# One written order for all engines: lists of pieces for the ramp and for each batch of an attention and feed-forward kernel

## The chip, the cores and the metric

The kernel runs on one core of a Trainium2 chip. The metric is the time of one execution on the device in microseconds (us), lower is better. An execution is repeated a few times, and medians and intervals are given. Times "in the trace" come from one profiled execution and count from the start of its span; the span is about 2 us shorter than the measured time of the same execution (before: 399.9 us of span, 401.66 us measured).

The engines are called by their names: TensorE (PE, with its weight loads PEld), VectorE (DVE), ScalarE (ACT), GpSimd (POOL, which here only issues loads), and SyncE (SP, which issues transposes by DMA and the stores).

## The reference

Block-causal attention for 8 batches, 8 heads, 576 positions and head dimension 64 (blocks of 64), then an RMS norm over the 512 concatenated channels and a gated feed-forward layer:

```python
scores = scale * np.matmul(q, k.transpose(0, 1, 3, 2))       # masked by blocks of 64
attn = np.exp(scores - max) / sum
x = np.matmul(attn, v)            # -> 4608 tokens x 512
xn = x / sqrt(mean(x * x) + 1e-6) * rms_g
g = xn @ w_gate                   # 512 -> 1536
out = (g * sigmoid(g) * (xn @ w_val)) @ w_out                # 1536 -> 512
```

Everything is float32 outside and bfloat16 in the matmuls.

## The kernel before

Attention of batch b runs on TensorE interleaved with the feed-forward layer of the batches before it, so that TensorE has other work while ScalarE computes exponentials. The feed-forward work lies in a queue of *pieces*: a gate piece, a value piece or a third of a down projection, each of 4 matmuls of 512 columns (or 8 of 256). A chunk of 512 tokens gives 36 pieces, and it enters the queue ("release") once its tokens are normalised and transposed.

The places that matter: batches 0 and 1 are loaded "wide" (many heads in one load) and transposed on TensorE; later batches are loaded by head and transposed by DMA. The norm of a batch is five squares (ScalarE), an inverse root of about a dozen small VectorE operations, five scales (VectorE), each followed by a DMA transpose into the chunk `XT`.

```python
def norm_squares(b, tiles): ...            # one ScalarE Square per tile, accum_out=ss
def norm_scale(b, tiles):
    def root(): ...                        # 1/sqrt by 3 Newton steps, 12 small VectorE operations
    def one(j, t):
        nc.vector.scalar_tensor_tensor(out=XS[:, j, :], in0=XN[:, t, :], scalar=rs[:, j:j + 1], in1=grow, ...)
        for i, (a, e) in enumerate(chunks):
            ...
            sp(nc.sync.dma_start_transpose(out=xt(i)[:, :, lo - a:hi - a], in_=XS[...]))
...
load_wide(0, 0, 0, 2); load_wide(0, 1, 0, 2)          # queries, keys of heads 0-1 of batch 0
load_wide(0, 0, 2, 4); load_wide(0, 1, 2, 4)
load_v_chunk(0, 0);    load_v_chunk(0, 1)
load_wide(0, 0, 4, H); load_wide(0, 1, 4, H)
...
for hp in range(HP):                                   # the ramp: batch 0, first 256 tokens
    tpose_wide(0, hp)
    early[hp].both(0)
    if hp > 1:
        early[hp - 2].values(0)
...
for s, sl in enumerate(slots):                         # one slot per batch and pair of heads
    ...
    budget = max(0, total - RESERVE) / (nxt - s) ...   # feed-forward pieces for this slot
    for i, f in enumerate(pieces):                     # scores and exponentials, values, ...
        if f: f()
        ...
        left = ffn(left + budget * shares[i] / sum(shares))
    for f in todo + aside + rels.pop(s, []) + pp + loads.pop(s, []):
        f()
```

TensorE, the load queue (POOL) and SyncE are chained to the order in which the program is written; VectorE and ScalarE are ordered by the framework's scheduler.

The softmax here doesn't subtract the row's maximum and nothing guards it: scores larger than these inputs give would overflow.

## Time and profile before

| | before |
|---|---|
| time, median of 4 runs | 400.72 us |
| first feed-forward matmul | 31.0 us |
| first transposes of batch 1 on TensorE | 43.6 us |
| first scores of batch 2 | 72.6 us |
| first scores of batch 3 | 108.1 us |
| one steady batch (first scores to first scores) | 39.66 us |

The page gives busy tenths of 40 slices of 10 us each, for TensorE, for the clock that it was granted, and for the DMA engines:

```profile
PE   2559978986999999999999999999999999999996
PEclk9999999989899999999999999999999999999999
DMA  9999999999979997999899785590050032002002
```

TensorE is full from about 110 us on; what can be won lies before. The DMA engines are busy without a break for the first 110 us. The timeline of TensorE, before (start us, duration us, engine, line, operation, count, and in brackets the idle time just ahead of it and who ended it):

```profile
6.64 1.50 PE L195 MATMUL f<-ident,HT 96*64 96x96 bf16 x24 [6.64 <-DMA HT<-in_q_dram]
...
30.95 1.89 PE L89 MATMUL f<-XT,WG 128*128 128x256 bf16 x8
...
43.63 0.70 PE L195 MATMUL f<-ident,HT 96*64 96x96 bf16 x24
...
72.60 0.61 PE L89 MATMUL s<-QKT 64*128 64x512 bf16 x6
```

The second line is the first feed-forward piece, the third begins batch 1's transposes, the fourth is batch 2's first scores.

### The profile page before, as it was taken

To read this page: it belongs to the slowest core of one execution; us is meant where nothing else is said; L and a number is where in the kernel's file an instruction comes from. 1 tells how busy PE (TensorE), PEld (TensorE's weight loads), DVE (VectorE), ACT (ScalarE), POOL (GpSimd) and SP (SyncE) were. 2 spreads that over 40 slices of the span, in tenths; PEclk is the share of its full clock that TensorE was granted. 3 is DMA by queue.
4 is the path that set the end of the run, shared out by engine and by line. 5 is a ranking of instruction groups with operands and counts; after the bars stand their busy time and mean duration, and the time that the engine had idled before them with its cause. 6 is when DMAs were issued, how large, how long until landed. Compare 5 with 4: busy or idle time off the path is not lost.

```text
span 399.9 us, 7708 instructions
## 1 busy us (share of the span) xinstructions
PE 367.2 (92%) x2924; PEld 187.5 (47%) x2924; DVE 259.3 (65%) x664; ACT 208.7 (52%) x369; POOL 138.0 (35%) x192
## 2 busy tenths in 40 slices
PE   2559978986999999999999999999999999999996
PEld 1337745752444444454445444544445444444442
DVE  6763895665578568846884679467947873742850
ACT  1256666783567466746673667366734622323321
POOL 8743497898059305840692061000000000000000
PEclk9999999989899999999999999999999999999999
DMA  9999999999979997999899785590050032002002
GB/s 119 191 203 186 188 82 163 171 111 131 197 47 88 168 177 49 78 126 223 54 87 171 167 53 36 112 183 2 11 130 29 0 60 107 0 26 80 0 3 103
DMA packets 158597, 41.08 MB, mean 103 GB/s; under 512 B 145120, under 2 KB 153824, under 8 KB 158560
## 3 DMA queue, kind: packets, MB, share of 16 engines
q0 software_dynamic: 103840, 18.89, 61.7%
q1 hardware_dynamic: 54720, 21.70, 26.7%
q8 instruction: 23, 0.38, 0.4%
q14 instruction: 14, 0.11, 0.1%
HBM read 38.01 MB, written 9.44 MB: 119 GB/s over the span
## 4 chain that ended last, share of the span: by engine, by line
PE 70%; DVE 12%; ACT 11%; issue 3%; DMA 3%; POOL 1%; DVEq 0%; POOLq 0%; ACTq 0%
PE f L89 65%; ACT sq L340 5%; PE s L89 4%; ACT PT L258 3%; DVE th L426 2%; ACT th L425 2%; DVE HT L432 2%; DMA HT<-in_k_dram 2%; DVE QK L198 2%; DVE XN L306 1%; DMA XT<-XS 1%; DVE XS L356 1%; POOL HT L80 1%; DVE PT L268 1%; DVE y L320 1%
## 5 line engine op out<-in xcount | busy, mean ns | idle before, releaser
L89 PE MATMUL f<-XT,WG 128*128 128x512 bf16 (+1 forms) x480 | 112.9, 363 | 3.7 <-DMA XT<-XS 2.3
L89 PE MATMUL f<-XT,WV 128*128 128x512 bf16 (+1 forms) x480 | 113.2, 364 | 0.0
L425 ACT ACTIVATE th<-f 128x512 f32<-128x512 f32 x108 | 64.2, 596 | 84.2 <-PE f L89 76.4
L426 DVE SCALAR_TENSOR_TENSOR th<-th,f 128x512 f32<-128x512 f32 x108 | 74.0, 685 | 52.0 <-ACT th L425 51.2
L89 PE MATMUL f<-WO,HT 128*128 128x512 bf16 x432 | 99.7, 379 | 1.8 <-DVE XN L306 1.5
L258 ACT ACTIVATE PT<-s 128x1024 bf16<-128x1024 f32 x88 | 86.9, 1023 | 10.8 <-PE s L89 10.7
L432 DVE TENSOR_TENSOR HT<-th,f 128x512 bf16<-128x512 f32 x108 | 74.1, 686 | 8.8 <-PE f L89 1.8
L89 PEld LDWEIGHTS <-WG 128*128 128x128 bf16 x480 | 45.4, 99 | 47.8 <-issue 6.4
L80 POOL DMA_DIRECT2D VN<-in_v_dram x48 | 38.7, 854 | 82.9 <-PE f L89 76.8
L89 PEld LDWEIGHTS <-WV 128*128 128x128 bf16 x480 | 45.1, 99 | 44.1 <-issue 4.0
L89 PEld LDWEIGHTS <-HT 128*128 128x128 bf16 x432 | 39.8, 98 | 46.3 <-issue 2.9
L446 ACT ACTIVATE ob<-f 128x512 f32<-128x512 f32 x36 | 21.5, 597 | 71.7 <-PE f L89 69.7
L80 POOL DMA_DIRECT2D QKN<-in_q_dram x60 | 49.0, 816 | 5.0 <-DMA WO<-in_moe_w_out_dram 3.4
L80 POOL DMA_DIRECT2D QKN<-in_k_dram x60 | 48.7, 812 | 5.1 <-DMA WO<-in_moe_w_out_dram 2.1
L89 PEld LDWEIGHTS <-PT 128*128 128x128 bf16 x960 | 40.1, 100 | 20.2 <-DVE PT L268 4.9
L89 PE MATMUL f<-VN,PT 128*128 128x65 bf16 x960 | 44.1, 198 | 4.8 <-DVE PT L268 4.0
L268 DVE MEMSET PT<- 64x64 uint32 (+1 forms) x124 | 12.8, 114 | 44.1 <-ACT PT L258 39.9
L306 DVE TENSOR_TENSOR XN<-f,rd 128x320 f32<-128x320 f32 (+2 forms) x64 | 31.2, 489 | 1.3
L359 DVE SCALAR_TENSOR_TENSOR XS<-XN,y,grow 128x512 bf16<-128x512 f32 x35 | 24.9, 745 | 0.7
L340 ACT ACTIVATE sq<-XN 128x512 bf16<-128x512 f32 x40 | 25.0, 625 | 0.3
L89 PE MATMUL s<-QKT 64*128 64x512 bf16 (+4 forms) x240 | 22.5, 298 | 1.0 <-ACT PT L258 1.0
L89 PEld LDWEIGHTS <-QKT 64*128 64x128 bf16 (+1 forms) x264 | 10.4, 95 | 25.1 <-issue 22.2
(41 smaller groups left out, 139.3 us busy)
## 6 DMA issues: line engine op xcount, KB each, us to landing
out_dram<-ob SPq DMA_DIRECT2D x36, 256.0 KB, 2.6
VN<-in_v_dram POOLq DMA_DIRECT2D x32, 128.0 KB, 4.2
QKN<-in_k_dram POOLq DMA_DIRECT2D x48, 64.0 KB, 3.7
QKN<-in_q_dram POOLq DMA_DIRECT2D x48, 64.0 KB, 3.5
WG<-in_moe_w_gate_dram POOLq DMA_DIRECT2D x4, 384.0 KB, 10.8
WV<-in_moe_w_val_dram POOLq DMA_DIRECT2D x4, 384.0 KB, 11.5
WO<-in_moe_w_out_dram POOLq DMA_DIRECT2D x2, 768.0 KB, 10.6
XT<-XS SPq DMA_TRANSPOSE x39, 3.5
```

Source lines behind the costliest of these rows:

```text
L80: return chain("POOL", nc.gpsimd.dma_start(**kw))
L89: pe(nc.tensor.matmul(dst, w, r, start=start, stop=stop))
L198: nc.vector.tensor_copy(out=T[:, n, :].rearrange("p (j s) -> p j s", s=SLOT), in_=t[:, 0:S].rearrange("p (s j) -> p j s", s=SLOT))
L258: nc.scalar.activation(out=PT[:, a0:a0 + T4], in_=st, func=AF.Exp, scale=SM_SCALE)
L268: nc.vector.memset(blk[:, :, 0:BLK], 0.0)
L306: nc.vector.tensor_tensor(out=xn_tiles[self.b][:, t0:t0 + n, f0:f0 + m * D].rearrange("p t (h d) -> p h t d", h=m), in0=xv[:, :, :, 0:D], ...
L340: nc.scalar.activation(out=sq, in_=XN[:, t, :], func=AF.Square, accum_out=ss[:, j:j + 1])
L359: nc.vector.scalar_tensor_tensor(out=XS[:, j, :], in0=XN[:, t, :], scalar=rs[:, j:j + 1], in1=grow, op0=ALU.mult, op1=ALU.mult)
L425: nc.scalar.activation(out=th, in_=pg, func=AF.Tanh, scale=0.5)
L426: nc.vector.scalar_tensor_tensor(out=th, in0=th, scalar=1.0, in1=pg, op0=ALU.add, op1=ALU.mult)
L432: nc.vector.tensor_tensor(out=ht, in0=gates.pop((i, k)), in1=pv, op=ALU.mult)
L446: nc.scalar.mul(out=ob, in_=po, mul=0.5)
```

## The change

The intent is to fix the order of every engine, and to shorten the ramp. Slots and budgets go; the program is a text of tokens per batch, in which `F` is one feed-forward piece, `A0`, `B1`, ... are sessions of scores and exponentials, `V00`, ... values, `q0`-`q4`, `r`, `c0`-`c4` the squares, root and scales (each with its transpose) of the batch before, `z` its release, `l` one prefetch load and `p` one transpose of queries and keys. VectorE and ScalarE are chained as TensorE was.

```diff
+    RAMP = """
+    F T0 F T1 F T2 F E0 E1 M1 M0 F T3 E2 e0 E3 e2 D00 F e1 F D10 e3 n0 Z n1 nr F D01 Z D02 nx M2 L0
+    D11 F K0 Z M3 Z F nt K2 F F D03 F K1 a0 F F D22 F D13 D12 D20 F D21 F F D23 a1 D31 t0 D30 K3
...
+    SECOND = """
+    F v0 p v1 A0 F q4 F q1 p F F q0 F F q2 F B1 F F q3 F F F F r c2 F F l c0 c1 V00 c3 F V01 C1 F F
+    F F F l l l F F F A2 F V10 p l F V11 l B3 l c4 z F F F p l C3 F F l l F l F F l l V20 V21 l F F
+    """
+    STEADY = """          (the same text as SECOND)
+    END = """
+    v1 v0 F q4 q3 F F F q0 F q2 q1 F r F c3 c4 F F c1 F F c2 c0 z
+    """
...
+    class Ordered:
...
+            return lambda *a, **kw: chain(self.key, f(*a, **kw))
+    dve = Ordered("DVE", nc.vector)
+    act_ = Ordered("ACT", nc.scalar)
...
-            nc.vector.tensor_copy(out=T[:, n, :]...            # query and key copies
+            copy = act_.copy if n == 0 else dve.tensor_copy    # queries to ScalarE
...
-    load_wide(0, 0, 0, 2)
     load_wide(0, 1, 0, 2)
+    load_wide(0, 0, 0, 2)
...
+    for h in (4, 6):
+        load_wide(0, 1, h, h + 2)
+        load_wide(0, 0, h, h + 2)
+    for c in range(NC):
+        load_v_chunk(0, c)
```

Batch 0's first squares and scales are split between VectorE and ScalarE, its root loses one operation, two large clears become small ones, and four matmuls on zeros (`Z`) are put into the ramp.

## The prediction

> **What bounds the kernel now.** TensorE, everywhere but at the front. The windows view has it busy 39.5 to 39.7 of each 40 us from 160 to 360 us, and the chain of waits repeats every 39.67 us per batch. Priced at the warm rates of the trace (a 512-column matmul 0.216 us apart, a values matmul 0.041), the work between 110 and 390 us loses only some 5 us. By the same count (an estimate from those durations) about 43 us are lost before 110 us: 23 until the first feed-forward matmul at 31.0 us, 10 more until batch 2's scores at 72.6, 10 more until 110. Only these can be won; some 4 us at the end (last eviction and store) stay.
>
> Inside them the timeline shows: the first load landing at 6.60 us; query and key copies of 0.76 us, two in a row on VectorE, before each score; squares of batch 0 on ScalarE behind exponentials (22.7 to 24.6), a root of twelve small VectorE operations mixed with masks (24.7 to 28.3), scales to 29.5; 128x256 feed-forward matmuls in eights at 1.89 us until 36 us where later ones take 1.05. The Trainium skill, "TensorE: Matmul & The Clock Gate", Part 1, says an idle TensorE is clocked at half rate and needs about 3.4 us of activity to warm; these numbers agree, and the granted clock falls to 0.50 in 84 to 86 us after waits for exponentials.
>
> **What the change does.** It removes no matmul and adds four 512-column ones (zeros, about 1 us, in idle time). Half of the 16 query/key copies go to ScalarE; the two 1.47 us clears become small ones; batch-0 squares are split over VectorE and ScalarE, the root loses one operation and its interruptions, scales split over two engines. Key loads go first, in two-head pieces, values after them. All engine orders become fixed. Feed-forward pieces per batch: 21 in the ramp, 25 in batch 2 (its queue runs dry for 12 list entries until batch 1 is released), 36 after, 11 plus 87 at the end.
>
> **Size, step by step** (estimates from the durations above). Batch 0's last early values finish near 18 instead of 21.9 us; squares 0.8, root about 2.1, scale 0.6, transposes and copies 1.5: first feed-forward matmul at 23.5 us instead of 31.0, so -7.5. From there the loads limit: wide keys of batch 1 land at 38.5 us and down-projection weights at 45.5 and 49.7 in the old trace, with queues that hold the same bytes; the transposes of batch 1 begin near 38.5 instead of 43.6, and batch 2 near 65 instead of 72.6. Batch 2 without feed-forward pieces in its middle is bound by ScalarE's exponentials of about 1 us: I expect 6 us lost there instead of 10. Steady batches: the period changes by under 0.5 us. Nearly all of the ramp's gain is on the critical path, since everything after is TensorE in order. Sum: about -12 us, so 388.5 us (range 382.5 to 394.5). Chances: faster 0.84, same 0.14, slower 0.02.
>
> **What would show it.** First feed-forward matmul at 22 to 26 us; batch-1 transposes at 37 to 41; batch 2's first scores at 62 to 68; a thin stretch of TensorE in batch 2; batch period 39.2 to 39.9; the tail after the last scores at the warm 0.86 us per four matmuls. DMA busy share of the ramp unchanged.
>
> **What would make it wrong.** Values of batch 0 landing later than about 14 us, behind all keys and queries; the fixed order putting a late operation before an urgent one on VectorE or ScalarE; a cold clock in batch 2's thin stretch; or steady batches that gain (or lose) a microsecond each.

## More of the kernel before

SyncE's own timeline in batch 2, before:

```profile
91.28 7.70 SPq L367 DMA_TRANSPOSE XT<-XS  x6
99.34 1.25 SPq L208 DMA_TRANSPOSE QKT<-QKN  x1
```

and of the group of instructions that touch `XT` between 60 and 110 us, before, the wait and the time from issue to landing of the six transposes:

```profile
  DMA XT<-XS: 2.3, 1
...
DMA to landing us min/median/max: 4.3/4.6/5.1
```

TensorE waits 2.3 us for the normalised batch 1. (Next to each transpose, loads of queries and keys were in flight here too; those of the values of batch 3 had landed by 89.4 us.)

## The result

| | before | after |
|---|---|---|
| time, median of 4 runs each | 400.72 us | 396.57 us (396.10 to 396.88) |
| ratio | | 0.9894, 95% interval 0.9874 to 0.9915 |
| first feed-forward matmul | 31.0 | 23.9 |
| first transposes of batch 1 | 43.6 | 38.6 |
| first scores of batch 2 | 72.6 | 68.4 |
| first scores of batch 3 | 108.1 | 109.4 |
| steady batch | 39.66 | 39.00 |

The change is about 1% faster, clear of the noise but under 2%, a third of what was predicted, and outside the range.

The page, after, in the same three rows:

```profile
PE   2888879973999999999999999999999899999996
PEclk9999999995999999999999999999999999999999
DMA  8999999999999999977999691760140031002002
```

The first slices are fuller, and a hole has opened in the ninth and tenth (79 to 99 us), with the clock at half speed in the tenth. The timeline of TensorE, after:

```profile
6.81 4.46 PE L224 MATMUL f<-ident,HT 96*64 96x96 bf16 x72 [6.81 <-DMA HT<-in_k_dram]
...
23.93 1.96 PE L117 MATMUL f<-XT,WG 128*128 128x256 bf16 x8
...
38.62 0.70 PE L224 MATMUL f<-ident,HT 96*64 96x96 bf16 x24
...
68.40 0.61 PE L117 MATMUL s<-QKT 64*128 64x512 bf16 x6
...
95.21 0.59 PE L117 MATMUL f<-XT,WG 128*128 128x512 bf16 x1 [7.51 <-DMA XT<-XS]
96.02 1.06 PE L117 MATMUL f<-XT,WG 128*128 128x512 bf16 x2 [0.22 <-issue]
96.87 1.91 PE L117 MATMUL f<-XT,WV 128*128 128x512 bf16 x4
...
100.59 1.03 PE L117 MATMUL f<-XT,WV 128*128 128x512 bf16 x4
```

TensorE has run all fifteen pieces that the queue still held and most of batch 2's attention by 87.7 us, and then waits 7.51 us for the transposed activations of batch 1. The pieces after the wait take 1.91 us for four matmuls until the clock is back, where later ones take 1.03. SyncE's timeline and the `XT` group (60 to 110 us), after:

```profile
82.01 1.19 SPq L414 DMA_TRANSPOSE XT<-XS  x1
83.30 0.53 SPq L512 DMA_DIRECT2D out_dram<-ob  x1
83.92 6.50 SPq L414 DMA_TRANSPOSE XT<-XS  x4
```

```profile
  DMA XT<-XS: 7.5, 1
...
DMA to landing us min/median/max: 4.1/7.6/8.7
```

The transposes are issued 9 us earlier than before (82.0 against 91.3), but the slowest now takes 8.7 us to land instead of 5.1. TensorE's next chunk needs the first four of the six: the fourth was issued at 86.99 us and landed at 95.07, and the wait ended at 95.21.

**Where the gain went.** The two kernels do not do the same work between the same marks, so the lead has to be corrected for it: one feed-forward piece (4 weight loads) is 0.863 us at the warm pace, and two groups of values are 1.07 us. At batch 2's first scores both have done 152 feed-forward weight loads, and the changed kernel has two value groups more. At batch 3's it has 20 weight loads (5 pieces) and two value groups more; at the last values, 8 weight loads (2 pieces) more.

| mark | before | after | extra work done, after | lead of after |
|---|---|---|---|---|
| first scores of batch 2 | 72.60 | 68.40 | 1.1 us | 5.3 us |
| first scores of batch 3 | 108.12 | 109.40 | 5.4 us | 4.1 us |
| first scores of batch 7 | 266.80 | 265.38 | 5.4 us | 6.8 us |
| last values | 308.89 | 303.40 | 1.7 us | 7.2 us |
| end of span | 399.9 | 394.7 | none | 5.2 us |

So the ramp wins 5.3 us, batch 2 loses 1.2, the four steady batches from 3 to 7 win 2.7, batch 7 itself 0.4, and the end loses 2.0.

The end: the last list puts the root and the scales of batch 7 on VectorE between gate and value pieces, whose products then stand behind them (timeline of TensorE, after):

```profile
312.87 1.02 PE L117 MATMUL f<-XT,WG 128*128 128x512 bf16 x4 [0.65 <-DVE th L111]
...
314.79 1.02 PE L117 MATMUL f<-XT,WV 128*128 128x512 bf16 x4 [0.90 <-DVE HT L111]
```

The kernel before has no wait of this size there.

### The profile page after: what moved, and what is told of

Read it like the earlier page. It is cut to its first block, busy times and chain, and to the rows that moved or that the text cites. A ratio compares the mean times of both kernels' runs of the same rounds, so it can differ in the third digit from the quotient of the medians.

```text
span 394.7 us, 7685 instructions
## 1 busy us (share of the span) xinstructions
PE 361.1 (91%) x2888; PEld 187.5 (48%) x2928; DVE 254.5 (64%) x658; ACT 210.0 (53%) x365; POOL 139.1 (35%) x194
## 4 chain that ended last, share of the span: by engine, by line
PE 73%; DVE 10%; ACT 7%; issue 4%; DMA 3%; POOL 1%; DVEq 0%; POOLq 0%; ACTq 0%
PE f L117 69%; ACT PT L111 5%; PE s L117 4%; DVE th L111 2%; DMA XT<-XS 2%; DVE XS L111 2%; DVE HT L111 2%; DMA HT<-in_q_dram 1%; DVE XN L111 1%; ACT ob L111 1%; DVE QK L111 1%; DVE a L111 1%; POOL HT L97 1%; ACT th L111 1%; DVE PT L111 1%
## 5 line engine op out<-in xcount | busy, mean ns | idle before, releaser
L117 PE MATMUL f<-XT,WV 128*128 128x512 bf16 (+1 forms) x473 | 111.5, 362 | 1.7 <-DVE HT L111 0.9
L111 ACT ACTIVATE PT<-s 128x1024 bf16<-128x1024 f32 (+2 forms) x100 | 95.5, 991 | 19.9 <-PE s L117 19.6
L117 PE MATMUL f<-WO,HT 128*128 128x512 bf16 x420 | 97.4, 379 | 1.1 <-DVE HT L111 0.5
L117 PEld LDWEIGHTS <-WV 128*128 128x128 bf16 x480 | 46.6, 99 | 48.5 <-issue 4.8
L117 PEld LDWEIGHTS <-HT 128*128 128x128 bf16 x432 | 40.6, 98 | 48.6 <-issue 1.6
L111 DVE MEMSET PT<- 64x64 uint32 (+3 forms) x128 | 13.2, 116 | 51.9 <-ACT PT L111 49.6
L117 PEld LDWEIGHTS <-PT 128*128 128x128 bf16 x960 | 34.5, 98 | 13.6 <-DVE PT L111 5.4
L117 PE MATMUL f<-VN,PT 128*128 128x65 bf16 x960 | 37.0, 194 | 3.8 <-DVE PT L111 3.8
L111 DVE SCALAR_TENSOR_TENSOR XS<-XN,y,grow 128x512 bf16<-128x512 f32 x38 | 27.0, 746 | 0.6
L111 ACT ACTIVATE sq<-XN 128x512 bf16<-128x512 f32 x38 | 24.0, 632 | 0.9 <-DVE XN L111 0.7
```

The lines of the kernel that those rows point to most:

```text
L111: return lambda *a, **kw: chain(self.key, f(*a, **kw))
L117: pe(nc.tensor.matmul(dst, w, r, start=start, stop=stop))
```

## The experiments

Fourteen variants ran, all of the changed kernel and all with a correct result; each is compared with the kernel before in its own rounds. By a 2% line only e5 and e14 are clearly faster than the kernel before; e2, e10, e12 and e13 lie on the line, and the others count as the same. Differences between variants are therefore read from the marks in their traces, each of one execution. Theory A was that the wait in batch 2 comes from the list: the norm of batch 1 is spread behind the fifteen pieces. Rival B was that the transposes land slowly because prefetch loads of later batches are in the DMA engines at the same time. Rival C was that ScalarE binds batch 2.

### e1: another list for batch 2

```diff
     SECOND = """
-    F v0 p v1 A0 F q4 F q1 p F F q0 F F q2 F B1 F F q3 F F F F r c2 F F l c0 c1 V00 c3 F V01 C1 F F
...
+    v0 p v1 q4 q1 F q0 F q2 F q3 A0 F r F p c2 F c0 F c1 F c3 B1 F V00 F V01 C1 F F F
+    F V10 A2 V11 F F l l l B3 c4 z V20 V21 l C3 F F l l F p F l F l F l F l p F l F l F l l
```

> Only batch 2's list is rewritten: the squares, root and scales of batch 1 come first, the 15 feed-forward pieces that are left are spread over and after them. Theory A (TensorE runs out of queued pieces at 87.7 us because the norm chain of batch 1 is spread behind them and ends late): the 7.5 us wait for the transposed activations shrinks below 2 us, batch 3's first scores move from 109.4 to about 103, and the time falls by 5 to 7 us to about 390 us. Rival B (the wait is a slow landing of the transposes among the prefetch loads): transposes still take 5 to 8 us to land and the gain is under 3 us. Rival C (batch 2 is bound by ScalarE's exponentials whatever the order): idle time of TensorE only moves within the batch, gain under 1 us.

Measured: 395.97 us, ratio 0.9895. The 7.5 us wait was gone, yet nothing was won: waits of 1.77, 1.38, 1.07 and 1.33 us appeared between 75 and 85 us, the clock fell in the middle of the batch, and batch 3 began at 108.97 us. The first transpose was issued only 1.1 us earlier (80.90 us), so this list was not the clean test of theory A that I wanted. It shows what rival C foresaw for the time, that idle time moved within the batch, though three of the four waits were on VectorE's gate and value products, not on exponentials (the fourth is put down to a load of values). It also shows what rival B foresaw: the transposes still took 5.9 us to land in the median (3.3 to 6.9), and the gain was under 3 us.

### e2: batch 2's prefetch loads held back

```diff
-    ... F A2 F V10 p l F V11 l B3 l c4 z F F F p l C3 ...
+    ... F A2 F V10 p F V11 B3 c4 z F w l l l l l l l F F p l C3 ...      (no l before z)
+             "w": lambda: gate.append(last["PE"]),
     def pool_dma(**kw):
-        return chain("POOL", nc.gpsimd.dma_start(**kw))
+        ins = chain("POOL", nc.gpsimd.dma_start(**kw))
+        if gate:
+            tc.add_manual_dep(ins.ins, gate.pop().ins.name, sync, reason="gate")
+        return ins
```

The order of all other work is kept. The first load after `w` waits for the first feed-forward matmul after the release.

> The list of batch 2 keeps its order, but its prefetch loads (values of batch 3, queries and keys of batch 4) wait until the first feed-forward matmul after the release. Theory B (landing time among the loads makes the 7.5 us wait): the transposes land about 2.6 us after issue instead of 4 to 8, the wait shrinks to 3 to 4 us, time falls by 3 to 4 us. Theory A (the scales of batch 1 are simply issued late, the last needed one near 87 us): wait shrinks by 1 to 2 us at most, time within 2 us of the changed kernel.

Measured: 390.68 us, ratio 0.976. The `XT` group between 60 and 110 us and the line of TensorE at the end of the wait, e2:

```profile
DMA to landing us min/median/max: 2.3/3.1/4.2
```

```profile
89.56 1.86 PE L121 MATMUL f<-XT,WG 128*128 128x512 bf16 x4 [2.18 <-DMA XT<-XS]
```

The transposes are issued within 1 us of their times in the changed kernel (81.54 and from 83.44 us, against 82.01 and from 83.92), but land in 3.1 us in the median instead of 7.6; the wait falls from 7.51 to 2.18 us, and batch 3 begins at 103.04 instead of 109.40 us. The table of windows gives the DMA engines a share of 2.57 between 86 and 90 us in the changed kernel and 0.37 in e2 (that view adds up the times of all packets, so it can pass 1). Theory B accounts for most of the wait: with the order of compute untouched, 6 us came back. What is left fits theory A: the last loads landed at 83.9 us, but the fourth transpose was issued only at 86.06 us and landed at 89.43. The Trainium skill, "DMA: Bandwidth & Descriptors", section "Issuing engines are not separate DMA queues", says that DMAs of SyncE, ScalarE and GpSimd run on the same 16 engines and interleave. This agrees: holding back loads that GpSimd issues cut the median landing time of transposes that SyncE issues from 7.6 to 3.1 us.

### e3: the last list

```diff
     END = """
-    v1 v0 F q4 q3 F F F q0 F q2 q1 F r F c3 c4 F F c1 F F c2 c0 z
+    v1 v0 F q4 F q3 F q0 F q2 F q1 F F F F F F F F r F c3 F c4 F c1 c2 c0 z
```

> Only the last list is rewritten: the root of batch 7 is put after all gate and value pieces, so that no root or scale stands between them on VectorE. Theory: the stalls of 0.65, 0.90 and 0.52 us at 312 to 320 us come from gate products queued behind the root and scales on VectorE; they go, and time falls by 1.5 to 2.3 us. Rival: with the root later, the last chunks' transposes land too late and a wait of 1 us or more on them appears, net gain under 0.7 us.

Measured: 394.53 us, ratio 0.9864. From the last values to the end of the span took 89.94 us instead of 91.29: 1.35 us won, just under the expected 1.5. The waits of 0.65, 0.90 and 0.52 us are gone; one of 0.86 us is new, the last value product standing behind the root:

```profile
317.40 2.77 PE L117 MATMUL f<-WO,HT 128*128 128x512 bf16 x12 [0.86 <-DVE HT L111]
```

### e4: e1 and e3 together

> Both list changes. If the two costs are separate and both on TensorE's path, the gains add: 7 to 9 us, about 388 us, which is where the prediction stood. If the later work absorbs what batch 2 gives, less than the sum.

Measured: 393.77 us, ratio 0.984. It is e3's gain alone, as e1 gave nothing.

### e5: e2 and e3 together

> The gated loads of e2 and the last list of e3 together. If the two costs lie in series on TensorE's path, the gains add: 6 us and 2 us below the changed kernel, so about 388 us, and the profiled span about 385.5 to 386.5 us. If part of one was only moved, the sum falls short by over 1 us.

Measured: 389.15 us, ratio 0.9719, and a profiled span of 387.3 us. Batch 3 begins at 103.39 us as in e2, and the end takes 89.94 us as in e3. In the traces the gains add.

### e6: the root of batch 2's list earlier, loads as they were

```diff
-    ... F q2 F B1 F F q3 F F F F r c2 F F l c0 c1 V00 ...
+    ... F q2 F q3 F B1 F r c2 F F F F F F l c0 c1 V00 ...
```

> Loads not gated; in batch 2's list only the last square goes before the exponentials of the second session and root and first scale go right after them. Theory (transposes issued before the value loads of batch 3, which start near 83 us, land fast): first transpose issued near 80 us instead of 82, landing within 4 us, the wait of 7.5 us shrinks to 3 to 5 us, gain 2 to 4 us. If only the congestion of the loads counts and two microseconds of earlier issue do not escape it: transposes land at the same time as before, near 95 us, gain under 1 us.

Measured: 396.76 us, ratio 0.9899, wait 8.43 us. It missed its own premise: on VectorE the root stood behind the masks of the second session, which wait for its exponentials, and the first transpose went out at 82.54 us, no earlier than in the changed kernel. It says nothing about earlier issue; e11 repeats it properly.

### e7: VectorE and ScalarE not chained

```diff
     class Ordered:
-            return lambda *a, **kw: chain(self.key, f(*a, **kw))
+            return f
```

> The lists stay, but VectorE and ScalarE are no longer chained to the written order; TensorE, the load queue and the transposes' queue keep theirs. If the fixed order of VectorE and ScalarE gave the steady batches their 38.99 us in place of 39.66, the period goes back above 39.3 us and the time rises by 2 to 6 us over the changed kernel. If TensorE's list alone gave it, the period stays within 0.15 us of 38.99.

Measured: 398.40 us, ratio 0.995. The lists alone give a *slower* steady batch, 40.3 to 40.6 us, than the kernel before (39.66), and the written order brings it to 39.00. The reason shows in the waits of TensorE between 146 and 300 us, e7:

```profile
PE f L117 <- DVE th L489: 4.3, 4, 1.1
PE f L117 <- DVE HT L495: 1.0, 4, 0.2
```

Once per batch TensorE waits 1.1 us for a gate product, for the scheduler had put the last steps of the root and a scale ahead of it on VectorE. The changed kernel has no wait at all in that view between 148 and 300 us, and the kernel before has four of about 0.4 us. In the ramp it is the other way round: without the chain, batch 2's first scores come at 65.4 us, not 68.4. The written order pays in the steady batches and costs in the ramp.

### e8: no matmuls on zeros

```diff
-             "Z": lambda: mm(fbank(), zeros[:, 0:P], zeros), ...
+             "Z": lambda: None, ...
```

> The four matmuls on zeros are left out. They stand in idle time before 23 us, and the first sixteen feed-forward matmuls ran at the slow pace (0.24 us per 256 columns) all the same, so I expect the same time within 0.5 us. If they warm TensorE's clock earlier than the rest would, the slow pace lasts 1 to 3 us longer and the time rises by 1 us or more.

Measured: 396.90 us, ratio 0.9893, the same as the changed kernel. The first feed-forward matmul is at 24.07 us, and the third piece takes 1.44 us instead of 1.22 for its eight matmuls. The zeros are worth nothing measurable.

### e9: the first loads in the old order

```diff
-    load_wide(0, 1, 0, 2)
     load_wide(0, 0, 0, 2)
+    load_wide(0, 1, 0, 2)
...
-    for h in (4, 6):
-        load_wide(0, 1, h, h + 2)
-        load_wide(0, 0, h, h + 2)
-    for c in range(NC):
-        load_v_chunk(0, c)
+    load_v_chunk(0, 0)
+    load_v_chunk(0, 1)
+    load_wide(0, 0, 4, H)
+    load_wide(0, 1, 4, H)
+    load_v_chunk(0, 2)
+    load_v_chunk(0, 3)
```

> Only the issue order of the first loads is put back: queries before keys, heads 4 to 7 in one load each, two value loads ahead of them. If the loads by need carry the earlier first feed-forward matmul, it moves from 23.9 us to 26 us or later and the whole ramp (batch 2's first scores at 68.4) with it. If the norm and the split copies carry it, it stays below 25 us; batch 2 starts within 1 us of 68.4 either way if the wide loads of batch 1 near 38 us set the pace after.

Measured: 399.42 us, ratio 0.9982: the whole gain is gone. The timeline of TensorE, e9:

```profile
13.52 1.17 PE L224 MATMUL f<-ident,HT 96*64 96x96 bf16 x24 [3.58 <-DMA HT<-in_k_dram]
...
27.36 1.96 PE L117 MATMUL f<-XT,WG 128*128 128x256 bf16 x8
```

TensorE stands 3.58 us in front of the third pair of heads, and everything after is 3.4 us late, up to 5.9 us at batch 2 (74.32 us). Part of it is returned in the wait of batch 2, which is 5.4 us instead of 7.5. So the loads by need are worth 3.4 of the 7.0 us at the first feed-forward matmul; by elimination the other half belongs to the shorter norm, the split copies and the small clears, which no run separated. The expectation that batch 2 would start within 1 us of 68.4 either way failed: batch 1's wide loads had landed at 37.4 us, but its transposes on TensorE began only at 42.4, so those loads did not set the pace in this run.

### e10: VectorE and ScalarE unchained in the ramp only

```diff
-            return lambda *a, **kw: chain(self.key, f(*a, **kw))
+            return lambda *a, **kw: chain(self.key, f(*a, **kw)) if written else f(*a, **kw)
...
         d = batch_steps(b)
+        if b > 1:
+            written.append(b)
```

> VectorE and ScalarE are unchained in the ramp alone, chained from batch 2 on. In the wholly unchained run batch 2's first scores came at 65.4 us instead of 68.4, but a steady batch took 40.57 us. If the two are separate: batch 2's first scores within 1 us of 65.4, steady period 38.99, the 7.5 us wait at the transposes kept or longer (the loads and transposes still collide), time 0 to 3.5 us below the changed kernel. If the chain is what pays in the ramp too: no earlier start, no gain.

Measured: 393.02 us, ratio 0.9815. Batch 2's first scores come at 65.81 us, the steady batches take 38.99 us except the first (39.83), and the wait is 5.56 us, shorter than I expected. Ramp and steady batches are separate, and the better order for each can be had.

### e11: root and scales in front of the second session, loads as they were

```diff
-    ... F q2 F B1 F F q3 F F F F r c2 F F l c0 c1 V00 c3 ...
+    ... F q2 F q3 F r c2 c0 c1 B1 F F F F F F F l V00 c3 ...
```

> Loads not gated. In batch 2's list the last square, the root and three scales go before the exponentials of the second session, where the queue holds only down projections that need no VectorE. e6 did not issue the transposes earlier; this one should, first at about 78 to 79.5 us instead of 82. Theory (transposes collide with loads of values of batch 3 from 83 us on): three of the four needed ones land before 88 us, the wait falls below 4 us, gain 3 to 5 us. If the collision is with any prefetch load: they still take 5 us or more each to land and the wait stays over 5 us.

Measured: 395.79 us, ratio 0.988, wait 6.74 us. Three transposes were issued at 80.70, 81.99 and 83.29 us and landed by 88.9, but the fourth needed one (issued 85.77) landed only at 94.60, while loads of batch 3's values were in flight until 94.75. Its landing times in the same view as above are

```profile
DMA to landing us min/median/max: 4.4/6.0/8.8
```

The expectation for "any prefetch load" came in for the wait, which stays over 5 us, and only in part for the landings: the first two took 4.4 and 4.7 us. The first issue (80.70 us) was also later than the 78 to 79.5 that I had wanted, so this test is weaker than planned; e14 is the clean one.

### e12: e2's gate, e10's ramp, e11's list and a still later root at the end

The edits of those runs, and in the last list `r` two pieces later than in e3.

> Candidate: ramp unchained, root early in batch 2 with gated loads, last list with the root after all gates and values. If all gains add: 3 us (ramp), 6 to 7.5 us (wait gone), 1.4 to 2 us (end) below the changed kernel: 384 to 387 us. Over 388 us: one of them is taken back by another.

Measured: 391.76 us, ratio 0.9785, worse than e5. Two things took it back. The still later root made TensorE wait 2.04 us for the last transposes at 319.7 us. And although batch 2 began at 65.09 us and its transposes were issued from 77.14 us on, the fourth landed at 88.56 us, much as in e2 (89.43) and e5 (89.49), so that batch 3 began at 103.09 us as there. The `XT` group (60 to 110 us) and TensorE's wait (68 to 104 us), e12:

```profile
DMA to landing us min/median/max: 2.8/4.6/6.3
```

```profile
PE f L122 <- DMA XT<-XS: 4.3, 1, 4.3
```

### e13 and e14: the loads of batch 3's queries and keys held back too

Why e2, e5 and e12 meet at the same point was still open. The traces give two different reasons. In e2 and e5 the last loads of batch 3's queries and keys had landed by 84.1 us, and the fourth transpose was issued only at 86.06 and 86.55 us. In e12 it was issued at 82.22 us, but such loads were in flight until 88.63. e13 is e5 with these nine loads (a tail and eight heads) moved behind the gate, and with them one `p` that needs them (all later loads move nine places too); e14 has e10's ramp and e11's list besides.

```diff
     RAMP: the last nine l left out
-    ... V10 p F V11 B3 c4 z F w l l l l l l l F F p l C3 ...
+    ... V10 F V11 B3 c4 z F w l l l l l l l l l p p l l l l l F F C3 ...
```

> e5 with the query and key loads of batch 3 also held until the first feed-forward matmul after the release. If these loads hold the transposes back, each lands within 3 us of its issue, the wait of 1.8 us in e5 falls below 1 us and batch 3 starts 1 to 2 us earlier, unless its own queries and keys now come too late (a wait at batch 3's first scores would show it): 387 to 389.5 us. If they do not: as e5.

> The same with the ramp unchained and the root early. If the loads of batch 3 were what held the transposes at 89 us in e12: the last needed one lands by 85 us, the 4.3 us wait shrinks below 1 us, batch 3's first scores come at 98 to 100.5 us instead of 103.1, time 384 to 387 us. If the transposes are slow without any prefetch load near them, the wait stays over 3 us and batch 3 stays at 102 us or later.

Measured, e13: 391.12 us, ratio 0.9767, but its six runs fall in two groups, 388.1 to 389.3 and 393.0 to 393.9, so its time decides nothing. Its trace does not show the expected change: the transposes land in 2.6 us in the median against 2.8 in e5, the fourth in 2.9 us in both, and the wait is 1.51 us instead of 1.76, as the loads had landed before in e5 already. New is a wait of 1.80 us at batch 3's own queries and keys, which now come late; batch 3 follows batch 2 after 34.8 us in both.

Measured, e14: 387.94 us (384.90 to 389.43), ratio 0.9681. The `XT` group and TensorE's waits between 80 and 104 us, e14:

```profile
DMA to landing us min/median/max: 2.3/2.4/4.0
```

```profile
PE s L121 <- DMA QKT<-QKN: 1.8, 1, 1.8
PE f L121 <- DMA XT<-XS: 1.8, 1, 1.8
```

The transposes now land 2.4 us after issue in the median, the fourth at 86.83 us, and batch 3 begins at 100.93 us, 2.2 us before e12. The fourth was issued at 82.8 us, as in e12 (82.2), and took 4.0 us instead of 6.3: in e12 the loads of batch 3 had held it back, and the ramp's gain comes through in part. It fell short of my numbers (wait 1.8 us instead of under 1, batch 3 at 100.9 instead of at most 100.5, time 1 us above the range) because holding these loads back costs 1.8 us at batch 3. After the wait for `XT` the first piece takes 1.02 us at once: the clock did not fall (granted clock 1.00 in this run, 0.985 in the changed kernel). That is the trace of one execution; the six fall in two groups here too, 384.9 to 386.7 and 389.2 to 389.4 us, it is of the faster one, and what parts the groups stays open. e14 beats both kernels, by 3.2% over the one before; against e5 (2.8%) the intervals overlap.

## Why the prediction was wrong

Its mechanism was right up to the first feed-forward matmul; the sum failed in batch 2, and smaller terms were wrong on both sides. Predicted were 7.6 us of lead at batch 2 and 4 more within it; the corrected lead was 5.3 us, then 1.2 less; the steady batches and batch 7 added 3.1, and the end took 2.0.

- **First feed-forward matmul: right.** Predicted 23.5, measured 23.9 us. Batch 1's transposes: predicted 38.5, measured 38.6 us, the number partly by luck: the load that was to set it landed at 37.9, and the 1.58 us that TensorE waits just before are put down to VectorE's masks (`DVE PT`). Unchained, in e10, TensorE does wait there for the load (1.57 us, until 38.03). e9 shows that the loads by need carry half of the gain at the first feed-forward matmul.
- **Batch 2's first scores: predicted 65, measured 68.4 us.** I had let the load of batch 1's keys set the pace from 38.5 us on and expected the rest of the ramp to run faster than before. From the transposes of batch 1 it took 29.8 us against 29.0 before, the two value groups of 1.07 us included. The changed kernel's written order on VectorE and ScalarE cost about 3 us there: unchained, the ramp reached batch 2 at 65.4 (e7) and 65.8 us (e10). As I wrote it, the danger was "the fixed order putting a late operation before an urgent one"; I gave it no number.
- **Batch 2: the step that failed.** The prediction says "I expect 6 us lost there instead of 10" and names ScalarE's exponentials as the bound. By the same count of work the changed kernel gained nothing in this batch and lost 1.2 us of its lead. Exponentials were not the bound (TensorE's waits for them after 82 us sum to 1.5 us): 7.5 us went into one wait for transposes by DMA (and another 2 to 3 us, an estimate from four matmuls at 1.91 instead of 1.03 us until 99 us, into the slow clock after it, a danger that the prediction named without a number). I had seen that the queue would run dry, and had seen the DMA engines busy to the end of the ramp, but I did not put the two together: the transposes were moved 9 us earlier, into a stretch where the prefetch loads had not moved. Values of batch 3 are issued at 83.0 to 87.1 us after and land at 89.0 to 94.8; before, they were issued at 79.3 to 86.3 and had landed by 89.4, ahead of the transposes. e2 settled it by moving only loads.
- **Steady batches: predicted change under 0.5 us, measured 0.67 us each.** The changed kernel no longer has the wait for a gate product, which was 0.36 us per batch before; where the other 0.3 us come from is not shown. e7 shows that the lists gain this only with VectorE and ScalarE in written order: 40.3 to 40.6 us unchained.
- **The end: predicted unchanged, measured 2.0 us lost**, of which e3 won back 1.35 by moving the root behind the gate and value pieces.
- **The zeros: right**, they cost and gave nothing.

The Trainium skill, "TensorE: Matmul & The Clock Gate", Part 1, on which the prediction leaned, says that an idle TensorE falls to half rate after about 3.4 us and needs about as much activity to warm up. The half rate agrees, the times fit less well. In the changed kernel the trace's clock records grant half rate from 89.28 to 99.52 us, from 1.6 us after TensorE stopped at 87.7. In the ramp TensorE was at work with gaps below 0.8 us from 6.8 us on, and the first two feed-forward pieces still ran at half pace, until 27.4 us (the granted clock reads 1.00 there, so only the pace shows it). And the length of a wait alone does not decide: after 2.18 us in e2 and 1.76 us in e5 the matmuls were slow, after 1.79 us in e14 and 1.51 us in e13 they were not.

What stays open: how the norm and the copies share the other half of the ramp's gain, which operation on VectorE or ScalarE costs the ramp its 3 us, why e13 and e14 run at two speeds, and whether a list exists that fills batch 2 without any wait.

## What to carry to other kernels

When a change makes compute reach a DMA sooner, look up what else is in the DMA engines at that moment: prefetch loads that cost little where they were can sit in front of a transfer that TensorE waits for. Test it by holding the loads back behind one later instruction, with all compute in its old order. In this kernel a fixed order on VectorE and ScalarE won 1.3 to 1.6 us in every steady batch and cost about 3 us in the one-off ramp, so check the scheduler's own order for each part.

## What the Trainium skill lacked or had wrong

- "DMA: Bandwidth & Descriptors", section "DMA Transpose (X-bar)": it gives no figure for how a DMA transpose slows when plain loads share the engines. Here transposes of up to 128x512 bfloat16 landed in 2.4 us (median, e14) with no prefetch load in flight but beside the last, and in 7.6 us (8.7 at most, the changed kernel) among such loads.
- "TensorE: Matmul & The Clock Gate", "Part 4: PE-mode transpose", says that the full clock does not engage for transposes on TensorE. Here 24 transposes of 96 columns took 1.17 us in the cold ramp and 0.70 us between warm matmuls at 38.6 us: they do run at the faster clock, once other work has raised it. The page adds that they don't count as work for the clock in the same way, and that fits: 72 of them back to back, 4.46 us from 6.81 us on, did not raise it, as the 24 after them at 11.95 us still took 1.17 us.
- The same page, Part 1, gives in its table an idle window of about 3.4 us as what lowers the clock; only for cycling through PSUM banks does it name frequent short gaps, without their length. In e2 a wait of 2.18 us, after a batch with short gaps, was followed by four matmuls at 1.86 us instead of 1.03. In the kernel before, half rate was granted from 83.50 to 86.91 us, though no wait of TensorE in the 8 us ahead was longer than 1.02 us. In the clock records every half-rate stretch but the one at the very end of a span lasted 3.41, 6.83 or 10.24 us.
